# A squared-ReLU MLP on one core: other load order, transposes and transfer sizes at the start

## The chip, the cores and the metric

The kernel runs on one core of one Trainium2 chip. The metric is the device time of one launch in microseconds. The times before are eight runs with a median of 291.09 us (290.92 to 291.54).

## What is computed

```python
B, S, D, F = 1, 2048, 576, 4608      # all inputs bf16
h = jnp.einsum("bsd,df->bsf", x, w1) + b1
r = jnp.where(h > 0, h, 0)
h = r * r
out = jnp.einsum("bsf,fd->bsd", h, w2) + b2
```

So each of 2048 rows of x (576 columns) goes through w1 (576 x 4608), a bias, ReLU, a square, w2 (4608 x 576) and a second bias.

## The kernel before

The 2048 rows are worked in four blocks `sb` of 512 rows. TensorE contracts over partitions, so x is wanted transposed: `xT_blk[sb]` holds nine windows of 128 partitions x 512 rows. Windows O to O+3 hold the four full slices of 128 columns, E3 the last 128 columns (448 to 575). `dup_windows` (L117 to L120) copies them with partitions 0 to 63 and 64 to 127 exchanged, so that every slice of 64 columns is found in both halves of the partitions; VectorE does it in two copies.

The hidden columns (36 tiles of 128) are split. The first four tiles (G = 4) are done by `a_full`, with w1 held as `w1n` (four chunks k of 128 rows x 512 columns) and `w1n8` (the last 64 rows of w1). The other 32 are done by `a_rows` in 16 steps j; each step runs two matmuls of 64 rows side by side, nine times (L188, L190), from `w1_h`, which holds two column halves h = 0 and 1 in partitions 0 to 63 and 64 to 127. After a PSUM bank is full, `evac_h` takes it: ScalarE adds b1 (`b1T`) and applies ReLU (L176), VectorE squares (L177). When two blocks are done, `phase_t` computes the last 128 output columns transposed (L270), and `phase_b` the first 448 (L289), both from `w2_sb`.

Only block 0 makes its own transposes, on TensorE, since it must start at once. Blocks 1 to 3 are transposed by DMA (`load_xT`).

The start, in the order of the code: seven warm matmuls on constants (L63, 3200 columns in all); x row tiles and w1n chunks are loaded, x tiles 1 and 2 from ScalarE's queue, the rest from SyncE's (L71 to L92); POOL makes `ident`, clears `b1_rows` and loads b1 and the end of b2 with its own DMAs (L95 to L102); ScalarE loads its activation table at L104. Then `a_full(0, "k_outer")` works in halves of 256 rows: `x_transpose(j, k)` (L145 to L149) puts a slice of x tile j into a PSUM bank, `x_copies(h)` (L151 to L159) brings one half's five slices to SBUF (three copies on VectorE, two on ScalarE), and `part(h, k)` (L224 to L229) multiplies one slice of one half with four column tiles of w1n. The order of these calls (L231 to L250) is TensorE's order. `make_b1T` (L164 to L167) transposes b1 in between, and `pair` (L202 to L206) adds the last 64 rows of w1. Then `a_rows(0, 12, 1)` begins; at its step 12 the windows of block 1 are copied.

SyncE's queue runs in the order of the code as well: the w1 columns in pairs h = 0, 1 for the steps j in (0,1), (1,2), (2,4), ... (10,12), with w1n8 after the first pair; the transposed x of block 1; columns (12,14), (14,16); b2 spread to all partitions; w2 in six transfers of six row tiles; x of blocks 2 and 3. `keep` holds the written order on each engine. In the build, the DMAs from SyncE and ScalarE take eight semaphores in turn, so that each one from the ninth on is issued only when the eighth before it has landed.

PSUM has eight banks: four in the pool `ps_h` and four in `ps_o`. Before, the transposes of block 0 use six of them, two banks of which are used for both halves.

Of the kernel before, what the change touches and what calls it, by code (L numbers as in the profile page):

```python
# [11 lines left out]
BF16 = mybir.dt.bfloat16  # L12
FP32 = mybir.dt.float32
# [4 lines left out]
def kernel(  # L18
# [9 lines left out]
    nc = tc.nc  # L28
    keep = tc.keep_in_program_order
    P = 128  # L30
    H = 64
    x2 = x.flatten_outer_dims()
    out2 = out.flatten_outer_dims()
    S, D = x2.shape
    F = w1.shape[1]
    NFT = F // P
    NC = D // H
    NK = NC // 2
    G = 4
    GW = G * P  # L40
# [6 lines left out]
    DM = D - DT  # L47

    const = ctx.enter_context(tc.tile_pool(name="const", bufs=1))
    wpool = ctx.enter_context(tc.tile_pool(name="wpool", bufs=1))  # L50
# [5 lines left out]
    ps_h = ctx.enter_context(tc.tile_pool(name="ps_h", bufs=4, space=PSUM))  # L56
    ps_o = ctx.enter_context(tc.tile_pool(name="ps_o", bufs=4, space=PSUM))

    wps = ps_o.tile([P, 512], FP32, name="wps", tag="po")
    ones = nc.const_aps.tensor(1.0, [P, 512], BF16)  # L60
    WARM = [512] * 6 + [128]
    for i, n in enumerate(WARM):
        keep(nc.tensor.matmul(wps[:, 0:n], lhsT=ones[:, 0:P], rhs=ones[:, 0:n], start=True, stop=True))  # L63

    xs = const.tile([P, RT, D], BF16, name="x_sb")
    w1n = wpool.tile([P, NK, GW], BF16, name="w1n")
    w1n8 = wpool.tile([P, G // 2, P], BF16, name="w1n8")
    w1_h = wpool.tile([P, NC, FH], BF16, name="w1_h")
    w1_v = w1.rearrange("(c p) f -> p c f", p=H)

    def load_x(eng, rt):  # L71
        keep(eng.dma_start(out=xs[:, rt, :], in_=x2[rt * P:(rt + 1) * P, :]))

    def load_w1n(eng, k):
        keep(eng.dma_start(out=w1n[:, k, :], in_=w1[k * P:(k + 1) * P, 0:GW]))

    def load_w1n8(eng, h):
        src = w1[NK * P:D, 0:GW].rearrange("p (i h f) -> p i h f", h=2, f=P)
        keep(eng.dma_start(out=w1n8[h * H:(h + 1) * H, :, :], in_=src[:, :, h, :]))

    def load_w1(eng, h, j0, j1):
        keep(eng.dma_start(out=w1_h[h * H:(h + 1) * H, :, j0 * P:j1 * P],
                      in_=w1_v[:, :, GW + h * FH + j0 * P:GW + h * FH + j1 * P]))

    load_x(nc.sync, 0)
    load_x(nc.scalar, 1)
    load_w1n(nc.sync, 0)
    load_x(nc.scalar, 2)
    load_w1n(nc.sync, 1)
    load_x(nc.sync, 3)  # L90
    for k in range(2, NK):
        load_w1n(nc.sync, k)  # L92

    ident = const.tile([P, P], BF16, name="ident")
    make_identity(nc, ident[:])  # L95
    b1_rows = const.tile([P, P], BF16, name="b1_rows")
    nc.gpsimd.memset(b1_rows[:], 0.0)
    nc.gpsimd.dma_start(out=b1_rows[0:NFT, :], in_=b1.rearrange("(ft p) -> ft p", p=P))
    b2_col = const.tile([P, 1], BF16, name="b2_col")
    nc.gpsimd.dma_start(out=b2_col[:], in_=b2[DM:D].rearrange("(d o) -> d o", o=1))  # L100
    b2T = const.tile([P, 1], FP32, name="b2T")
    nc.gpsimd.tensor_copy(out=b2T[:], in_=b2_col[:])  # L102
    warm = const.tile([P, 1], FP32, name="warm")
    keep(nc.scalar.activation(out=warm[:], in_=nc.const_aps.tensor(0.0, [P, 1], FP32), func=ACT.Relu))  # L104

    E3, O, SPC, E = 0, 1, 5, 6
    LO_W = [O, O + 1, O + 2, O + 3, E, E + 1, E + 2, E3, SPC]
# [20 lines left out]

    w2_sb = wpool.tile([P, NFT, D], BF16, name="w2_sb")
    w2_view = w2.rearrange("(ft p) d -> p ft d", p=P)  # L130
    W2CH = 6

    def load_w2(c):
        keep(nc.sync.dma_start(out=w2_sb[:, c * W2CH:(c + 1) * W2CH, :], in_=w2_view[:, c * W2CH:(c + 1) * W2CH, :]))
# [3 lines left out]
    alloc_xT(0)  # L138
    xT0 = xT_blk[0]
    HS = SB // 2  # L140
    tb_po = [ps_o.tile([P, 2, HS], BF16, name="tb", tag="po") for _ in range(2)]
    tb_ph = [ps_h.tile([P, 2, HS], BF16, name="tb", tag="ph") for _ in range(4)]
    half_banks = [tb_ph, None]

    def x_transpose(j, k):  # L145
        h, q = divmod(j, 2)
        qc = slice(q * P, (q + 1) * P)
        bank, slot, c0 = (half_banks[h][k], 0, k * P) if k < NK else (half_banks[h][2], 1, D - P)
        keep(nc.tensor.transpose(bank[:, slot, qc], xs[:, j, c0:c0 + P], ident[:]))  # L149

    def x_copies(h):  # L151
        hc = slice(h * HS, (h + 1) * HS)
        for k in range(NK):
            src = half_banks[h][k][:, 0, :]
            if k % 2 == 0:
                keep(nc.vector.tensor_copy(out=xT0[:, O + k, hc], in_=src))  # L156
            else:
                keep(nc.scalar.copy(out=xT0[:, O + k, hc], in_=src))
        keep(nc.vector.tensor_copy(out=xT0[:, E3, hc], in_=half_banks[h][2][:, 1, :]))  # L159


    b1T = const.tile([P, NFT], FP32, name="b1T")

    def make_b1T():  # L164
        b1T_ps = ps_o.tile([P, P], BF16, name="b1T_ps", tag="po")
        keep(nc.tensor.transpose(b1T_ps[:], b1_rows[:], ident[:]))  # L166
        keep(nc.vector.tensor_copy(out=b1T[:], in_=b1T_ps[:, 0:NFT]))  # L167

# [26 lines left out]
    def a_full(sb, order):  # L195
        xT = xT_blk[sb]
        banks = []
        for g in range(G):
            pool, tag = (ps_o, "po") if g < 2 else (ps_h, "ph")
            banks.append(pool.tile([P, SB], FP32, name="pn", tag=tag))  # L200

        def pair(i, start, stop):  # L202
            keep(nc.tensor.matmul(banks[2 * i][:], lhsT=w1n8[0:H, i, :], rhs=xT[0:H, SPC, :],  # L203
                             start=start, stop=stop, skip_group_check=order == "k_outer"))
            keep(nc.tensor.matmul(banks[2 * i + 1][:], lhsT=w1n8[H:P, i, :], rhs=xT[H:P, E3, :],  # L205
                             start=start, stop=stop, skip_group_check=order == "k_outer"))  # L206

        def full(g, k, start, stop):
            keep(nc.tensor.matmul(banks[g][:], lhsT=w1n[:, k, g * P:(g + 1) * P], rhs=xT[:, O + k, :],  # L209
                             start=start, stop=stop))  # L210

        if order == "rows_first":
            for i in (1, 0):
                pair(i, True, False)
            for g in (2, 3, 0, 1):
                for k in range(NK):
                    full(g, k, False, k == NK - 1)
                evac_h(sb, banks[g], g)
        else:
            if order == "k_outer":  # L220
                tb_new = [ps_h.tile([P, 2, HS], BF16, name="tb", tag="ph") for _ in range(2)]
                half_banks[1] = tb_new + tb_po

                def part(h, k):  # L224
                    hc = slice(h * HS, (h + 1) * HS)
                    for g in range(G):
                        keep(nc.tensor.matmul(banks[g][:, hc], lhsT=w1n[:, k, g * P:(g + 1) * P],  # L227
                                              rhs=xT[:, O + k, hc], start=(h == 0 and k == 0), stop=False,
                                              skip_group_check=True))  # L229

                for j in range(2):  # L231
                    for k in range(NK):
                        x_transpose(j, k)
                for j in range(2):
                    x_transpose(j, NK)
                x_copies(0)
                part(0, 0)
                for k in range(NK + 1):
                    x_transpose(2, k)
                part(0, 1)  # L240
                part(0, 2)
                for k in range(NK + 1):
                    x_transpose(3, k)
                x_copies(1)
                dup_windows(0)
                part(0, 3)
                part(1, 0)
                make_b1T()
                for k in range(1, NK):
                    part(1, k)  # L250
            else:
                for g in (2, 3, 0, 1):
                    for k in range(NK):
                        full(g, k, k == 0, False)
            for i in (1, 0):
                pair(i, False, True)
                evac_h(sb, banks[2 * i], 2 * i)
                evac_h(sb, banks[2 * i + 1], 2 * i + 1)
# [35 lines left out]
    for (j0, j1) in [(0, 1), (1, 2), (2, 4), (4, 6), (6, 8), (8, 10), (10, 12)]:  # L294
        load_w1(nc.sync, 0, j0, j1)
        load_w1(nc.sync, 1, j0, j1)
        if j0 == 0:
            load_w1n8(nc.sync, 0)
            load_w1n8(nc.sync, 1)
    load_xT(1)  # L300
    for (j0, j1) in [(12, 14), (14, 16)]:
        load_w1(nc.sync, 0, j0, j1)
        load_w1(nc.sync, 1, j0, j1)
    keep(nc.sync.dma_start(out=b2_bc[:], in_=b2.partition_broadcast(P)))
    for c in (0, 3, 1, 4, 2, 5):
        load_w2(c)
    load_xT(2)

    alloc_hT(0)
    a_full(0, "k_outer")  # L310
    a_rows(0, 12, 1)
    alloc_hT(1)
# [47 lines left out]
```

## Time and profile before

| what | value |
|---|---|
| median of eight runs | 291.09 us |
| profiled execution, own time | 291.17 us |
| its span in the profile | 289.4 us (1.77 us of the time lie outside) |
| DMA, whole span | 16.52 MB, mean 57 GB/s |
| DMA share from 0 to 3.8 us, and to 4.9 | 0.55, then 0.93 |
| first row matmul (L188) | at 9.79 us |
| TensorE from 10 to 20 us | busy 10.00 us |
| w1 columns, 288 KB each | 14 issues, median 6.1 us to landing |
| w2, 864 KB each | 6 issues, median 9.9 us to landing |

The times inside the profile count from the start of its span. PE is TensorE, PEld its weight loads, DVE VectorE, ACT ScalarE, SP SyncE; an engine's name with a q is its sequencer, which issues DMAs. A line of the timeline has the start, the length, the engine, the line of the kernel, the operation, what it writes and reads, the number of instructions, and in brackets the idle time before them with what ended it. Matmul ends are modelled; the distance between two starts tells the rate.

### The profile page before, as it was taken

The page shows a single profiled execution, that of the slowest core. Times are in us where ns is not written, and L with a number is a line of the kernel's source. Part 1 is how long each engine was busy: PE and PEld are TensorE (multiplying, and loading weights), DVE is VectorE, ACT ScalarE, POOL GpSimd, SP SyncE. Part 2 cuts the span into 40 slices and gives each one's busy share as a digit, 9 for nine tenths or more (in the row PEclk, how much of TensorE's full clock was granted, in tenths as well). Part 3 has the DMA queues.
Part 4 walks back from the last instruction along what each step waited for, and adds up shares of the span by engine and source line. Part 5 has one row for each costly group of instructions (what it writes and reads, how often), then busy time and mean ns, then how long its engine had stood idle before and what let it go on. Part 6 is the DMA issues. An engine that isn't in the chain of part 4 may idle for free.

```text
span 289.4 us, 4699 instructions
## 1 busy us (share of the span) xinstructions
PE 285.3 (99%) x2032; PEld 139.4 (48%) x2032; DVE 78.6 (27%) x176; ACT 96.7 (33%) x154; POOL 2.3 (1%) x10
## 2 busy tenths in 40 slices
PE   8999999999999999999999999999999999999995
PEld 5544444444444555555544444444444455555554
DVE  1644544444500200000025444444440001100001
ACT  3666666766500000000027666666770000000000
POOL 3000000000000000000000000000000000000000
DMA  7999999200001100000000000000000110000000
GB/s 195 223 250 197 321 386 222 61 0 2 0 18 33 39 16 18 16 16 18 16 16 2 1 2 0 2 0 2 0 2 0 36 39 16 16 17 32 19 16 18
DMA packets 31638, 16.52 MB, mean 57 GB/s; under 512 B 15733, under 2 KB 31617, under 8 KB 31617
## 3 DMA queue, kind: packets, MB, share of 16 engines
q1 hardware_dynamic: 31264, 15.91, 21.6%
q10 hardware_dynamic: 288, 0.30, 0.4%
q8 instruction: 16, 0.26, 0.4%
q14 instruction: 6, 0.04, 0.0%
q0 software_dynamic: 64, 0.01, 0.0%
HBM read 11.36 MB, written 2.36 MB: 47 GB/s over the span
## 4 chain that ended last, share of the span: by engine, by line
PE 98%; DMA 1%; DVE 0%; issue 0%
PE ph L188 42%; PE po L289 38%; PE pt L270 11%; PE pn L209 4%; PE pn L227 1%; DMA x_sb<-in_x_dram 1%; PE tb L149 1%; PE ph L190 1%; PE pn L203 1%; DVE o_sb L291 0%; PE b1T_ps L166 0%; PE pn L205 0%
## 5 line engine op out<-in xcount | busy, mean ns | idle before, releaser
L188 PE MATMUL ph<-xTw,w_h 64*128 64x512 bf16 x576 | 124.6, 376 | 0.0
L190 PE MATMUL ph<-xTw,w_h 64*128 64x512 bf16 x576 | 124.6, 376 | 0.0
L289 PE MATMUL po<-w_sb,hT 128*128 128x448 bf16 (+2 forms) x612 | 109.4, 341 | 0.0
L176 ACT ACTIVATE r<-ph,b1T 128x512 bf16<-128x512 f32 x128 | 81.1, 685 | 41.6 <-PE ph L190 41.6
L188 PEld LDWEIGHTS <-w_h 64*128 64x128 bf16 x576 | 54.1, 94 | 68.1
L289 PEld LDWEIGHTS <-hT 128*128 128x128 bf16 x612 | 58.5, 98 | 51.0
L177 DVE TENSOR_TENSOR hT<-r 128x512 bf16<-128x512 bf16 x144 | 61.2, 426 | 75.8 <-ACT r L176 75.2
L190 PEld LDWEIGHTS <-w_h 64*128 64x128 bf16 x576 | 54.1, 94 | 0.0
L291 DVE TENSOR_TENSOR o_sb<-po,b_bc 128x448 bf16<-128x448 f32 (+2 forms) x17 | 10.2, 597 | 125.8 <-PE po L289 125.8
L270 PE MATMUL pt<-hT,w_sb 128*128 128x512 bf16 x144 | 31.4, 379 | 0.0
L176 ACT ACTIVATE r<-pn,b1T 128x512 bf16<-128x512 f32 x16 | 10.3, 688 | 61.0 <-PE pn L205 59.6
L270 PEld LDWEIGHTS <-w_sb 128*128 128x128 bf16 x144 | 14.1, 98 | 17.0
L273 ACT ACTIVATE oT<-pt,b2T 128x512 bf16<-128x512 f32 x4 | 2.8, 688 | 28.3 <-PE pt L270 28.3
L209 PE MATMUL pn<-xTw,w1n 128*128 128x512 bf16 x48 | 10.9, 379 | 0.0
L209 PEld LDWEIGHTS <-w1n 128*128 128x128 bf16 x48 | 4.5, 98 | 6.0 <-issue 0.8
L227 PE MATMUL pn<-xTw,w1n 128*128 128x256 bf16 x32 | 4.0, 272 | 0.0
L63 PE MATMUL wps<-const-bfloat16-1.0 128*128 128x512 bf16 (+1 forms) x7 | 2.8, 578 | 0.8 <-PEq L344 0.8
L227 PEld LDWEIGHTS <-w1n 128*128 128x128 bf16 x32 | 3.0, 99 | 0.3
L119 DVE COPY xTw<-xTw 64x2048 bf16<-64x2048 bf16 x4 | 2.8, 690 | 0.2
L156 DVE COPY xTw<-tb 128x256 bf16<-128x256 bf16 x4 | 1.1, 292 | 6.2 <-PE tb L149 6.2
L120 DVE COPY xTw<-xTw 64x2048 bf16<-64x2048 bf16 x4 | 2.8, 688 | 0.1
L149 PE MATMUL tb<-ident,x_sb 128*128 128x128 bf16 x20 | 2.3, 263 | 0.3 <-DMA x_sb<-in_x_dram 0.2
(23 smaller groups left out, 14.9 us busy)
## 6 DMA issues: line engine op xcount, KB each, us to landing
w_sb<-in_w_dram SPq DMA_DIRECT2D x6, 864.0 KB, 9.9
w_h<-in_w_dram SPq DMA_DIRECT2D x14, 288.0 KB, 6.1
out_dram<-o_sb SPq DMA_DIRECT2D x15, 112.0 KB, 1.7
w_h<-in_w_dram SPq DMA_DIRECT2D x4, 144.0 KB, 3.4
w1n<-in_w_dram SPq DMA_DIRECT2D x4, 128.0 KB, 3.3
out_dram<-ot SPq DMA_DIRECT2D x4, 128.0 KB, 2.0
x_sb<-in_x_dram ACTq DMA_DIRECT2D x2, 144.0 KB, 2.9
x_sb<-in_x_dram SPq DMA_DIRECT2D x2, 144.0 KB, 3.3
```

What stands on the lines that cost most here:

```text
L63: keep(nc.tensor.matmul(wps[:, 0:n], lhsT=ones[:, 0:P], rhs=ones[:, 0:n], start=True, stop=True))
L149: keep(nc.tensor.transpose(bank[:, slot, qc], xs[:, j, c0:c0 + P], ident[:]))
L176: keep(nc.scalar.activation(out=r[:], in_=bank[:], func=ACT.Relu, bias=b1T[:, ft:ft + 1], scale=1.0))
L177: keep(nc.vector.tensor_tensor(out=hTs[sb][:, ft, :], in0=r[:], in1=r[:], op=ALU.mult))
L188: keep(nc.tensor.matmul(bx[:], lhsT=w1_h[0:H, LO_C[i], jc], rhs=xT[0:H, LO_W[i], :], start=(i == 0), stop=(i == NC - 1)))
L190: keep(nc.tensor.matmul(by[:], lhsT=w1_h[H:P, UP_C[i], jc], rhs=xT[H:P, UP_W[i], :], start=(i == 0), stop=(i == NC - 1)))
L203: keep(nc.tensor.matmul(banks[2 * i][:], lhsT=w1n8[0:H, i, :], rhs=xT[0:H, SPC, :], start=start, stop=stop, skip_group_check=order == "k_o ...
L209: keep(nc.tensor.matmul(banks[g][:], lhsT=w1n[:, k, g * P:(g + 1) * P], rhs=xT[:, O + k, :], start=start, stop=stop))
L227: keep(nc.tensor.matmul(banks[g][:, hc], lhsT=w1n[:, k, g * P:(g + 1) * P], rhs=xT[:, O + k, hc], start=(h == 0 and k == 0), stop=False, s ...
L270: keep(nc.tensor.matmul(pt[:], lhsT=w2_sb[:, ft, DM:D], rhs=hT[:, ft, :], start=(i == 0), stop=(i == NFT - 1)))
L289: keep(nc.tensor.matmul(po[:, 0:d1 - d0], lhsT=hT[:, ft, jj * P:(jj + 1) * P], rhs=w2_sb[:, ft, d0:d1], start=(i == 0), stop=(i == NFT - 1)))
L291: keep(nc.vector.tensor_tensor(out=o_sb[:, d0:d1], in0=po[:, 0:d1 - d0], in1=b2_bc[:, d0:d1], op=ALU.add))
```

## The change

The x row tiles 0 and 1 are loaded in two column pieces each (0 to 255, and 256 to 575), on SyncE and ScalarE. Then w1n chunks go on SyncE and x tiles 2 and 3 on ScalarE in turn; chunk 3 goes on ScalarE. b1 is loaded from ScalarE's queue after its activation table; `b1_rows` is cleared by VectorE; the end of b2 is loaded from SyncE's queue after the w1 columns. Both halves of w1n8 now hold all 512 columns and are loaded before the first w1 columns. The transposes have four banks of their own, all in `ps_h`, and each slice is copied out as soon as its second row tile is transposed; two of the ten copies are on ScalarE. Block 0's four accumulators all lie in `ps_o`. The order on TensorE becomes: slices 0 and 1 of x tiles 0 and 1, then their other three slices, one `part`, x tile 2, one `part`, x tile 3, and the rest. The w1 columns (12,14) and (14,16) become one pair (12,16), and w2 comes in two transfers of 18 row tiles in place of six of six. There are six warm matmuls with 2816 columns in all.

```diff
-    wps = ps_o.tile([P, 512], FP32, name="wps", tag="po")
+    wps = ps_h.tile([P, 512], FP32, name="wps", tag="ph")
-    WARM = [512] * 6 + [128]
+    WARM = [512] * 5 + [256]
...
-    w1n8 = wpool.tile([P, G // 2, P], BF16, name="w1n8")
+    w1n8 = wpool.tile([P, GW], BF16, name="w1n8")
...
+    def load_x(eng, rt, c0=0, c1=D):
+        keep(eng.dma_start(out=xs[:, rt, c0:c1], in_=x2[rt * P:(rt + 1) * P, c0:c1]))
...
     def load_w1n8(eng, h):
-        src = w1[NK * P:D, 0:GW].rearrange("p (i h f) -> p i h f", h=2, f=P)
-        keep(eng.dma_start(out=w1n8[h * H:(h + 1) * H, :, :], in_=src[:, :, h, :]))
+        keep(eng.dma_start(out=w1n8[h * H:(h + 1) * H, :], in_=w1[NK * P:D, 0:GW]))
...
-    load_x(nc.sync, 0)
-    load_x(nc.scalar, 1)
-    load_w1n(nc.sync, 0)
-    load_x(nc.scalar, 2)
-    load_w1n(nc.sync, 1)
-    load_x(nc.sync, 3)
-    for k in range(2, NK):
-        load_w1n(nc.sync, k)
+    b1_rows = const.tile([P, P], BF16, name="b1_rows")
+    nc.vector.memset(b1_rows[:], 0.0)
+    for c0, c1 in [(0, 2 * P), (2 * P, D)]:
+        load_x(nc.sync, 0, c0, c1)
+        load_x(nc.scalar, 1, c0, c1)
+    for k in range(2):
+        load_w1n(nc.sync, k, k + 1)
+        load_x(nc.scalar, 2 + k)
+    load_w1n(nc.sync, 2, 3)
+    load_w1n(nc.scalar, 3, 4)
...
-    b1_rows = const.tile([P, P], BF16, name="b1_rows")
-    nc.gpsimd.memset(b1_rows[:], 0.0)
-    nc.gpsimd.dma_start(out=b1_rows[0:NFT, :], in_=b1.rearrange("(ft p) -> ft p", p=P))
-    b2_col = const.tile([P, 1], BF16, name="b2_col")
-    nc.gpsimd.dma_start(out=b2_col[:], in_=b2[DM:D].rearrange("(d o) -> d o", o=1))
-    b2T = const.tile([P, 1], FP32, name="b2T")
-    nc.gpsimd.tensor_copy(out=b2T[:], in_=b2_col[:])
     warm = const.tile([P, 1], FP32, name="warm")
     keep(nc.scalar.activation(out=warm[:], ...))
+    keep(nc.scalar.dma_start(out=b1_rows[0:NFT, :], in_=b1.rearrange("(ft p) -> ft p", p=P)))
+    for h in range(2):
+        load_w1n8(nc.sync, h)
...
-    W2CH = 6
+    W2CH = 18
...
-    tb_po = [ps_o.tile([P, 2, HS], BF16, name="tb", tag="po") for _ in range(2)]
-    tb_ph = [ps_h.tile([P, 2, HS], BF16, name="tb", tag="ph") for _ in range(4)]
+    tb = [[ps_h.tile([P, 4, HS], BF16, name="tb", tag="ph") for _ in range(2)] for _ in range(2)]
+    PLACE = [(0, 0), (0, 1), (1, 0), (1, 1), (0, 2)]
+    T_ORDER = [0, 1, 2, 3, NK]
+
+    def x_transpose(j, ks=T_ORDER):
+        h, q = divmod(j, 2)
+        hc = slice(h * HS, (h + 1) * HS)
+        for k in ks:
+            bank, slot = PLACE[k]
+            c0 = k * P if k < NK else D - P
+            keep(nc.tensor.transpose(tb[h][bank][:, slot, q * P:(q + 1) * P], xs[:, j, c0:c0 + P], ident[:]))
+            if q == 1:
+                w = O + k if k < NK else E3
+                if h == 1 and bank == 1:
+                    keep(nc.scalar.copy(out=xT0[:, w, hc], in_=tb[h][bank][:, slot, :]))
+                else:
+                    keep(nc.vector.tensor_copy(out=xT0[:, w, hc], in_=tb[h][bank][:, slot, :]))
...
-        b1T_ps = ps_o.tile([P, P], BF16, name="b1T_ps", tag="po")
+        b1T_ps = ps_h.tile([P, P], BF16, name="b1T_ps", tag="ph")
...
-            pool, tag = (ps_o, "po") if g < 2 else (ps_h, "ph")
+            pool, tag = (ps_o, "po") if g < 2 or order == "k_outer" else (ps_h, "ph")
...
-                for j in range(2):
-                    for k in range(NK):
-                        x_transpose(j, k)
-                for j in range(2):
-                    x_transpose(j, NK)
-                x_copies(0)
-                part(0, 0)
-                for k in range(NK + 1):
-                    x_transpose(2, k)
-                part(0, 1)
-                part(0, 2)
-                for k in range(NK + 1):
-                    x_transpose(3, k)
-                x_copies(1)
+                for ks in (T_ORDER[:2], T_ORDER[2:]):
+                    for j in range(2):
+                        x_transpose(j, ks)
+                for k in range(2):
+                    part(0, k)
+                    x_transpose(2 + k)
                 dup_windows(0)
-                part(0, 3)
+                for k in range(2, NK):
+                    part(0, k)
                 part(1, 0)
                 make_b1T()
...
     for (j0, j1) in [(0, 1), (1, 2), (2, 4), (4, 6), (6, 8), (8, 10), (10, 12)]:
         load_w1(nc.sync, 0, j0, j1)
         load_w1(nc.sync, 1, j0, j1)
-        if j0 == 0:
-            load_w1n8(nc.sync, 0)
-            load_w1n8(nc.sync, 1)
     load_xT(1)
-    for (j0, j1) in [(12, 14), (14, 16)]:
+    for (j0, j1) in [(12, 16)]:
         load_w1(nc.sync, 0, j0, j1)
         load_w1(nc.sync, 1, j0, j1)
+    b2_col = const.tile([P, 1], BF16, name="b2_col")
+    keep(nc.sync.dma_start(out=b2_col[:], in_=b2[DM:D].rearrange("(d o) -> d o", o=1)))
+    b2T = const.tile([P, 1], FP32, name="b2T")
+    nc.gpsimd.tensor_copy(out=b2T[:], in_=b2_col[:])
     keep(nc.sync.dma_start(out=b2_bc[:], in_=b2.partition_broadcast(P)))
-    for c in (0, 3, 1, 4, 2, 5):
+    for c in range(2):
         load_w2(c)
     load_xT(2)
```

More of the change, by code (lines that the diff above doesn't have):

```diff
@@ L66, with load_w1n @@
     w1n = wpool.tile([P, NK, GW], BF16, name="w1n")
-    w1n8 = wpool.tile([P, G // 2, P], BF16, name="w1n8")
+    w1n8 = wpool.tile([P, GW], BF16, name="w1n8")
     w1_h = wpool.tile([P, NC, FH], BF16, name="w1_h")
     w1_v = w1.rearrange("(c p) f -> p c f", p=H)
[L71 to L75, printed above, removed]
+    def load_x(eng, rt, c0=0, c1=D):
+        keep(eng.dma_start(out=xs[:, rt, c0:c1], in_=x2[rt * P:(rt + 1) * P, c0:c1]))
+    def load_w1n(eng, k0, k1):
+        src = w1[k0 * P:k1 * P, 0:GW].rearrange("(k p) f -> p k f", p=P)
+        keep(eng.dma_start(out=w1n[:, k0:k1, :], in_=src))
     def load_w1n8(eng, h):
-        src = w1[NK * P:D, 0:GW].rearrange("p (i h f) -> p i h f", h=2, f=P)
-        keep(eng.dma_start(out=w1n8[h * H:(h + 1) * H, :, :], in_=src[:, :, h, :]))
+        keep(eng.dma_start(out=w1n8[h * H:(h + 1) * H, :], in_=w1[NK * P:D, 0:GW]))
     def load_w1(eng, h, j0, j1):
@@ L140 @@
     HS = SB // 2
-    tb_po = [ps_o.tile([P, 2, HS], BF16, name="tb", tag="po") for _ in range(2)]
-    tb_ph = [ps_h.tile([P, 2, HS], BF16, name="tb", tag="ph") for _ in range(4)]
-    half_banks = [tb_ph, None]
-    def x_transpose(j, k):
+    tb = [[ps_h.tile([P, 4, HS], BF16, name="tb", tag="ph") for _ in range(2)] for _ in range(2)]
+    PLACE = [(0, 0), (0, 1), (1, 0), (1, 1), (0, 2)]
+    T_ORDER = [0, 1, 2, 3, NK]
+    def x_transpose(j, ks=T_ORDER):
         h, q = divmod(j, 2)
[L147 to L151, printed above, removed]
         hc = slice(h * HS, (h + 1) * HS)
-        for k in range(NK):
[L154 to L159, printed above, removed]
+        for k in ks:
[8 more added lines that the diff above has]
+                    keep(nc.vector.tensor_copy(out=xT0[:, w, hc], in_=tb[h][bank][:, slot, :]))
     b1T = const.tile([P, NFT], FP32, name="b1T")
     def make_b1T():
-        b1T_ps = ps_o.tile([P, P], BF16, name="b1T_ps", tag="po")
+        b1T_ps = ps_h.tile([P, P], BF16, name="b1T_ps", tag="ph")
         keep(nc.tensor.transpose(b1T_ps[:], b1_rows[:], ident[:]))
@@ L198, in a_full @@
         for g in range(G):
-            pool, tag = (ps_o, "po") if g < 2 else (ps_h, "ph")
+            pool, tag = (ps_o, "po") if g < 2 or order == "k_outer" else (ps_h, "ph")
             banks.append(pool.tile([P, SB], FP32, name="pn", tag=tag))
         def pair(i, start, stop):
-            keep(nc.tensor.matmul(banks[2 * i][:], lhsT=w1n8[0:H, i, :], rhs=xT[0:H, SPC, :],
+            keep(nc.tensor.matmul(banks[2 * i][:], lhsT=w1n8[0:H, 2 * i * P:(2 * i + 1) * P], rhs=xT[0:H, SPC, :],
                              start=start, stop=stop, skip_group_check=order == "k_outer"))
-            keep(nc.tensor.matmul(banks[2 * i + 1][:], lhsT=w1n8[H:P, i, :], rhs=xT[H:P, E3, :],
+            keep(nc.tensor.matmul(banks[2 * i + 1][:], lhsT=w1n8[H:P, (2 * i + 1) * P:(2 * i + 2) * P], rhs=xT[H:P, E3, :],
                              start=start, stop=stop, skip_group_check=order == "k_outer"))
@@ L220, in a_full @@
             if order == "k_outer":
-                tb_new = [ps_h.tile([P, 2, HS], BF16, name="tb", tag="ph") for _ in range(2)]
-                half_banks[1] = tb_new + tb_po
                 def part(h, k):
@@ L229, in part @@
                                               skip_group_check=True))
-                for j in range(2):
-                    for k in range(NK):
-                        x_transpose(j, k)
-                for j in range(2):
-                    x_transpose(j, NK)
-                x_copies(0)
-                part(0, 0)
-                for k in range(NK + 1):
-                    x_transpose(2, k)
-                part(0, 1)
-                part(0, 2)
-                for k in range(NK + 1):
-                    x_transpose(3, k)
-                x_copies(1)
+                for ks in (T_ORDER[:2], T_ORDER[2:]):
[4 more added lines that the diff above has]
+                    x_transpose(2 + k)
                 dup_windows(0)
-                part(0, 3)
+                for k in range(2, NK):
+                    part(0, k)
                 part(1, 0)
```

## The prediction

> **What bounds the kernel now.** I read the page first. TensorE is busy almost throughout, while the DMA queues and ScalarE have room:
>
> ```profile
> PE 285.3 (99%) x2032; PEld 139.4 (48%) x2032; DVE 78.6 (27%) x176; ACT 96.7 (33%) x154; POOL 2.3 (1%) x10
> ...
> PE 98%; DMA 1%; DVE 0%; issue 0%
> ```
>
> The change takes no row matmul, no L289 and no L270 away. What it can move is the head, before the w1 rows (L188) begin, or a load that the rows come to wait for. The chain of waits shows the head in order of time (start, length, what):
>
> ```profile
> 0.73 3.04 DMA x_sb<-in_x_dram
> 3.83 1.22 PE tb L149 x10
> 5.04 0.48 PE pn L227 x4
> 5.62 0.40 PE tb L149 x4
> 6.02 0.87 PE pn L227 x8
> 6.90 0.28 PE tb L149 x5
> 7.17 0.87 PE pn L227 x8
> ```
>
> TensorE waits for x to 3.83. The first ten transposes take 0.107 us each, the later five of L149 (6.90 to 7.17) only 0.056: the first ten run at half rate. From 4.92 the 128x256 matmuls start 0.109 us apart. The timeline gives the rest: TensorE idles from 5.38+ to 5.62 for a free bank, and again before 9.35, because VectorE's window copies (L119, L120) end at 9.22.
>
> ```profile
> 5.62 0.23 PEld L149 LDWEIGHTS <-x_sb 128*128 128x128 bf16 x4 [0.28 <-DVE xTw L159]
> ...
> 8.53 0.69 DVE L120 COPY xTw<-xTw 64x2048 bf16<-64x2048 bf16 x1
> ...
> 9.34 0.09 PEld L203 LDWEIGHTS <-w1n 64*128 64x128 bf16 x1 [0.21 <-issue]
> ```
>
> The last view is the timeline of SyncE beside the rows. Rows start at 9.79; each j takes 9 x 0.216 = 1.94 us, so j=2 starts at 13.68. It needs the w1 columns (2,4), which SP issues at 7.72 (h=0, partitions 0 to 63) and 8.40 (h=1, the other 64):
>
> ```profile
> 7.72 0.64 SPq L82 DMA_DIRECT2D w_h<-in_w_dram  x1
> 8.40 0.64 SPq L82 DMA_DIRECT2D w_h<-in_w_dram  x1
> ...
> 13.46 0.38 PE L190 MATMUL ph<-xTw,w_h 64*128 64x512 bf16 x1
> 13.58 0.09 PEld L190 LDWEIGHTS <-w_h 64*128 64x128 bf16 x1
> ```
>
> The DMA view of short windows gives 4.7 and 5.1 us to landing for those two, so 12.4 and 13.5. The weight load at 13.58 lies 0.12 behind its usual place: the chunk comes a tenth of a microsecond ahead of need. So the head has two bounds close together: TensorE's own work, and the supply of w1 columns (2,4). The next pair (issued 9.09 and 9.77) lands by about 15.7 and is needed at 17.56.
>
> **What the skill says.** "TensorE: Matmul & The Clock Gate", part on the HAM clock gate: the array starts at half clock, 107 against 56 ns for 128 columns, and turns to full after some 4 us of activity. The trace agrees: 0.107, then 0.056, and the turn lies at about 4.9, 4.1 us after the first warm matmul at 0.78. The page adds that the window runs freely, so the turn can shift. "DMA: Bandwidth & Descriptors", section on issuing engines: transfers from SP and ACT run on the same 16 DMA engines, so a second queue saves only issue time. The trace agrees in size: 0.40 to 0.47 us per issue. "ScalarE: Activation LUTs", on what a table load costs: 1283 ns, from a backing slot filled earlier. The trace has 1.28, so I take it as unaffected by DMA traffic.
>
> **The change, part by part.**
>
> *First x pieces.* Before, x tiles 0 and 1 (2 x 144 KB) are issued at 0.73 and landed by 3.77; packets flow from 1.76 and 0.27 MB are through by 3.0. Columns 0 to 255 of both are 131 KB, through by about 2.6 to 2.7 in the same traffic; with the 0.65 us from last packet to landing (3.77 less 3.1) that is 3.3. The warm matmuls shrink from 3200 to 2816 columns at 0.83 ns, ending the issue at about 3.2, so they don't stand in the way. Four transposes from 3.3 take 0.43. The other pieces (295 KB in all, plus 256 more packets than before) land at about 3.9, and six transposes end at 4.55. That is 0.35 earlier, all at half rate, so worth 0.18; the four following matmuls get another 0.3 us of half-rate time, worth 0.15.
>
> *Bank and window stalls.* Four own PSUM banks for the transposes remove the 0.24 at 5.38. The second transposes (j=3) come one group of four matmuls earlier, so L119/L120 end 0.6 before the pair needs them, where they were 0.13 late. VectorE now has eight copies at 0.29 and ScalarE two at 0.376; five copies of half 0 are hidden under the first two matmul groups. Sum of the head if nothing else comes late: 0.18 + 0.15 + 0.24 + 0.13 = 0.70, less about 0.2 of small gaps between pieces and waits for w1n = 0.5. Rows would start at 9.29.
>
> *Issue order and waits.* In both builds hardware DMAs take eight semaphores in turn, so each issue from the ninth on waits until the eighth before it has landed. Before, SP's own 0.4 to 0.7 us per issue was slower than that. Now the split makes two more transfers early, so w1n chunk 2 (SP) waits for x piece 0 (3.3, where it was issued at 2.65), chunk 3 (ACT) for x piece 1 (3.3, was 3.13). Queued behind chunk 2 are both w1n8 and all w1 columns; behind chunk 3 are the table load and b1.
> - Chunks 2 and 3: issued 3.3, landing 2.6 (nearest, less the cold start of the first x) to 3.4 us later (chunk 2 before), 5.9 to 6.7; needed at 6.17 and 6.6. I take 6.1; cost 0, at most 0.45.
> - w1n8 (64x512 twice, 131 KB instead of 64 KB): issued 3.9 and 4.35 after x's second pieces; each about 0.4. Landing 2.5 to 3.1 later, needed at 8.85: hidden.
> - w1 columns: j=0 h=0 at 4.8, h=1 waits for x tile 3 (ACT issue 2.1, plus 3.5, so 5.5). Then 0.68 per issue: j=1 at 6.2 and 6.85, columns (2,4) at 7.55 and 8.2. j=0 h=1 lands 3.6 later at 9.1, just in time. (2,4) h=1 lands 5.1 later at 13.3, while rows from 9.29 would need it at 13.17. So j=2 starts at about 13.45 instead of 13.68, and all later rows shift by that: a gain of 0.23, not 0.5.
> - b1: ACT issues chunk 3 to 3.7, table load to 5.0, warm activation 0.2, b1 at 5.25. A small load took 2.5 to 3.1 on SP in traffic; with an almost empty ACT ring I allow 1.9 to 3.3: 7.15 to 8.55. TensorE's in-order transpose (L166) needs it at 7.5, and twelve matmuls, the pairs and all rows are queued behind it. I take 7.5: no cost; the top costs 1.05 at that place. b2_col moves to the SP queue behind the last w1; it is used after 91 us.
>
> *Later loads.* Columns (12,16) come as one pair of 576 KB: issued at about 23.5, 1.18 MB at 250 to 390 GB/s (rates at 14-18 and 38-42) from 25.7, landing by 29.5 to 31.4; needed at j=12, 32.7. Hidden by 1.3 at the least. w2 in two transfers of 18 row tiles (the code has 18) moves the same bytes; before, SP was through issuing them at 38.4 and loads ended by 54, first use 75.9. Hidden by 20 us; b2_bc and the x transposes behind it are as far from use. POOL loses two DMAs of which none waits. Cost nothing, bounds plus or minus 0.05.
>
> Sum: the gain of 0.23 is seen at j=2. Against the profiled execution's own 291.17 (span 289.4 and 1.77 around it) that is 290.94. Its time lies 0.08 over the median 291.09, so I say 290.9. A measurement can tell about 0.2%, 0.58 us, from no change.
>
> **Rivals.**
> *Full gain.* Columns (2,4) land by 13.1 because the DMA engines start fuller; then 0.5 (up to 0.7) stays: 290.5. For it: DMA share was only 0.71 to 0.86 from 5.8 to 9.4. Against: the issue time of h=1 hardly moves (8.40 to 8.2). 0.25.
> *b1 comes late, slower.* The wait on x piece 1 holds ACT, then 1.28 and 0.2 stand ahead of b1's issue. It decides from a landing of about 7.95 on: then the rows start later than 9.79. At 8.55 rows start at 10.35, 0.55 later: 291.65. The same sign comes if x tile 3 lands at 6.0, since h=1 of column 0 waits for it. For it: w1n8's second half took 2.5 us and column 0 took 3.6 in that traffic. Against: ACT's ring holds nothing else by then. 0.22.
> *The change doesn't do what it says:* the x pieces land no earlier since packets, not bytes, set the start (256 packets either way). Then only the stalls vanish, and (2,4) sets the end anyway: 291.0, within the forecast's own range.
>
> **Numbers.** Forecast, 290.5 to 291.3 around 290.9: 0.53. Full gain 0.25, slower case 0.22. Below -0.58 lies about half of the full gain's case, 0.13; above +0.58 some four fifths of the slower case, 0.18, since a late b1 also pushes chunks; the rest, 0.69, is no measurable change. Range 290.4 to 291.6, which cuts the ends of both rivals.
>
> **What would show it.** First transpose at 3.2 to 3.4; no wait of L149 on VectorE; chunk 2's issue at about 3.3; b1's landing against its transpose; a gap on TensorE ahead of row j=2 ended by w_h; first row at 9.2 to 9.5. The forecast is wrong if a gap ahead of b1's transpose exceeds 0.4, if w1 columns after (2,4) or (12,16) end a gap, or if the clock turns far from 4.9.

## The result and the profile after

| | before | after |
|---|---|---|
| median | 291.23 us (290.87 to 291.75, 32 runs) | 293.19 us (292.23 to 295.48, 12 runs) |
| ratio to before | | 1.0066, 95% interval 1.0053 to 1.008 |
| profiled execution, own time | 291.17 us | 293.55 us |
| span | 289.4 us | 291.8 us |
| first transpose | 3.83 | 3.07 |
| first row matmul | 9.79 | 12.54 |

The kernel became slower by 1.9 us, against a forecast of 0.2 us less (290.9 against 291.09). The runs after lie in groups (292.2 to 292.8, 293.6, and one of 295.5), which those of before don't. The profiled execution, on which the lines below rest, is one of the middle group.

The first part of the page after, and its chain of waits up to the rows (start, length, what):

```profile
PE 286.6 (98%) x2031; PEld 140.1 (48%) x2031; DVE 79.5 (27%) x179; ACT 96.2 (33%) x152; POOL 0.9 (0%) x7
```

```profile
3.28 0.33 PE tb L149 x3
3.64 0.30 DVE xTw L155
4.29 0.30 DVE xTw L155
4.63 0.39 PE tb L149 x2
5.04 0.30 DVE xTw L155
5.38 0.37 PE tb L149 x2
5.75 0.85 PE pn L219 x4
6.61 0.53 PE tb L149 x5
7.14 0.85 PE pn L219 x4
8.14 0.30 DVE xTw L155
8.48 0.29 PE tb L149 x2
8.79 0.38 ACT xTw L153
9.49 1.31 PE pn L219 x12
```

Two things are new. Copies out of PSUM (L155 on VectorE, L153 on ScalarE) now stand in the chain between transposes; before, none did. And groups of four 128x256 matmuls take 0.85 us (0.213 each) at 5.75 and at 7.14, where they took 0.48 at 5.04 and 0.87 for eight at 6.02 before: the half rate lasts beyond 8 us instead of to 4.9. The timeline names the waits:

```profile
3.98 0.48 PE L149 MATMUL tb<-ident,x_sb 128*128 128x128 bf16 x3 [0.38 <-DVE xTw L155]
...
4.63 0.37 PE L149 MATMUL tb<-ident,x_sb 128*128 128x128 bf16 x2 [0.17 <-DVE xTw L155]
...
5.38 0.37 PE L149 MATMUL tb<-ident,x_sb 128*128 128x128 bf16 x2 [0.38 <-DVE xTw L155]
...
8.48 0.27 PE L149 MATMUL tb<-ident,x_sb 128*128 128x128 bf16 x2 [0.38 <-DVE xTw L155]
...
9.21 0.27 PE L149 MATMUL tb<-ident,x_sb 128*128 128x128 bf16 x2 [0.46 <-ACT xTw L153]
...
12.54 0.38 PE L183 MATMUL ph<-xTw,w_h 64*128 64x512 bf16 x1
```

The bracket counts from the modelled end of the transpose before. By the distance of starts, the five waits (ahead of 3.98, 4.63, 5.38, 8.48 and 9.21) take 0.59, 0.37, 0.59, 0.59 and 0.62 us, 2.76 in all. A transpose is done, the copy waits for it some 0.35, copies for 0.29, and only then may TensorE write the next slice into the same bank. "PSUM — Partial Sum Buffer", section on bank collisions, says why the build puts a wait there at all: TensorE writing and another engine reading the same bank at once is an error that the hardware doesn't arbitrate. The waits agree with that; no run here tried it without.

The sum of the head, from the first transpose to the first row: 9.47 us after, 5.96 before. Both hold 5.1 us of work at full pace (20 x 0.056, 32 x 0.109, 0.056, two pairs at 0.216). Half rate adds 1.65 after (16 transposes x 0.051, eight matmuls x 0.104) and 0.51 before (ten transposes); the rest, 2.7 after and 0.35 before, is idle. So the rows begin later by 2.4 (idle) + 1.1 (half rate) - 0.76 (transposes begin earlier) = 2.75. The span grows by 2.4, since the stretch from the last add to its end is 0.35 shorter.

### The profile page after: what moved, and what is told of

It is laid out like the page before. It is cut to its first block, busy times and chain, and to the rows that moved or that the text cites. A ratio compares the mean times of both kernels' runs of the same rounds, so it can differ in the third digit from the quotient of the medians.

```text
span 291.8 us, 4694 instructions
## 1 busy us (share of the span) xinstructions
PE 286.6 (98%) x2031; PEld 140.1 (48%) x2031; DVE 79.5 (27%) x179; ACT 96.2 (33%) x152; POOL 0.9 (0%) x7
## 4 chain that ended last, share of the span: by engine, by line
PE 98%; DVE 1%; issue 0%; ACT 0%
PE ph L183 42%; PE po L274 37%; PE pt L255 11%; PE pn L204 4%; PE pn L219 1%; PE tb L149 1%; PE wps L63 1%; PE ph L185 1%; PE pn L198 1%; DVE xTw L155 0%; ACT xTw L153 0%; DVE o_sb L276 0%; PE b1T_ps L161 0%; PE pn L200 0%
## 5 line engine op out<-in xcount | busy, mean ns | idle before, releaser
L255 PE MATMUL pt<-hT,w_sb 128*128 128x512 bf16 x144 | 31.4, 379 | 0.0
L149 PE MATMUL tb<-ident,x_sb 128*128 128x128 bf16 x20 | 3.3, 286 | 1.8 <-DVE xTw L155 1.3
L219 PE MATMUL pn<-xTw,w1n 128*128 128x256 bf16 x32 | 5.0, 309 | 0.0
L155 DVE COPY xTw<-tb 128x256 bf16<-128x256 bf16 x8 | 2.2, 291 | 6.6 <-PE tb L149 6.6
L149 PEld LDWEIGHTS <-x_sb 128*128 128x128 bf16 x20 | 2.3, 133 | 3.2 <-issue 2.0
L117 DVE COPY xTw<-xTw 64x2048 bf16<-64x2048 bf16 x4 | 2.8, 690 | 0.2
(20 smaller groups left out, 13.4 us busy)
```

The source lines that it names most:

```text
L149: keep(nc.tensor.transpose(tb[h][bank][:, slot, q * P:(q + 1) * P], xs[:, j, c0:c0 + P], ident[:]))
L255: keep(nc.tensor.matmul(pt[:], lhsT=w2_sb[:, ft, DM:D], rhs=hT[:, ft, :], start=(i == 0), stop=(i == NFT - 1)))
```

## The experiments

**Copies behind the transposes, and each side of the change alone.** Four kernels with one set of questions: is it the banks (theory A) or the loads (theory B), and does the clock follow from the gaps? The first expectation states both theories. Ratios are to the kernel before throughout, with a 95% interval behind them; first rows and turns of the clock are those of one profiled execution.

*e1_copies_after*, the kernel after with copies behind all transposes of a half:

```diff
-            if q == 1:
-                w = O + k if k < NK else E3
-                ...
+    def x_copies(h, ks=T_ORDER):
+        ...
                 for ks in (T_ORDER[:2], T_ORDER[2:]):
                     for j in range(2):
                         x_transpose(j, ks)
+                x_copies(0)
                 for k in range(2):
                     part(0, k)
                     x_transpose(2 + k)
+                x_copies(1)
```

> The kernel after, with one thing changed: the copies of a half are issued behind all ten transposes of that half, so that no transpose writes a PSUM bank that a copy still has to read. Loads, banks and the order of transposes and matmuls stay. Theory A (transposes wait for copies of the same bank, five times in the head, and the idle time also delays the turn of TensorE's clock): the waits are gone, the clock turns at about 5 us, the first row starts at 9.5 to 9.9 instead of 12.54, time 290.9 to 291.4. Theory B (the loads: the DMA issues that wait for a landing, and b1 behind the table load): nothing of that is changed, so the time stays within 292.2 to 293.7.

Measured: 292.78 (six runs, 291.82 to 293.35), ratio 1.0051 (1.0036 to 1.0067). The five waits are gone and the first row starts at 10.08, near what theory A said. Half rate ends early, between 3.4 and 3.6 by the pace of the transposes, but then TensorE waits for w1n chunk 0, which the x pieces ahead of it put from an issue at 1.20 to one at 1.65:

```profile
5.43 0.61 PE L222 MATMUL pn<-xTw,w1n 128*128 128x256 bf16 x4 [1.33 <-DMA w1n<-in_w_dram]
```

The time is not what theory A said; it lies in the range of theory B. A new wait stands in the rows. The waits in the window from 9 to 40 us, and the weight loads around step j=12:

```profile
PE ph L188 <- DMA w_h<-in_w_dram: 1.4, 1, 1.4
```

```profile
33.18 0.09 PEld L186 LDWEIGHTS <-w_h 64*128 64x128 bf16 x1
35.17 0.09 PEld L188 LDWEIGHTS <-w_h 64*128 64x128 bf16 x1 [1.90 <-DMA w_h<-in_w_dram]
```

That is the second half of columns (12,16). The weights come 1.78 late (35.17 against 33.39), and from row start to the last add this execution is 1.8 longer than before's. So theory A held for the bank waits of the head, and a second loss lay behind it.

*e2_loads_only*: the loads after, everything on TensorE and PSUM as before.

```diff
-    tb = [[ps_h.tile([P, 4, HS], ...) for _ in range(2)] for _ in range(2)]
+    tb_po = [ps_o.tile([P, 2, HS], BF16, name="tb", tag="po") for _ in range(2)]
+    tb_ph = [ps_h.tile([P, 2, HS], BF16, name="tb", tag="ph") for _ in range(4)]
...
+    x_transpose, x_copies and the order of a_full as before
```

> The loads and their order as after, shorter warm-up as after, but transposes, copies, PSUM banks and TensorE's order as before. Theory A: no wait on a shared bank, first row at 9.4 to 9.8, time 290.7 to 291.3. Theory B: as slow as after, 292.2 to 293.7.

Measured: 293.49 (291.87 to 293.68), ratio 1.0064 (1.0045 to 1.0083), first row at 12.35. Theory A wanted this kernel fast, as it has no bank waits; it is as slow as theory B said, so the loads have a loss of their own. Its timeline shows ScalarE's copies behind b1's issue:

```profile
5.12 0.74 ACTq L100 DMA_DIRECT2D b_rows<-in_b_dram  x1
...
5.90 0.65 ACT L156 COPY xTw<-tb 128x256 bf16<-128x256 bf16 x2 [0.98 <-DVE xTw L157]
```

*e3_transposes_only*: the loads before, transposes, banks and order after.

```diff
-    tb_po = [ps_o.tile([P, 2, HS], ...) for _ in range(2)]
-    tb_ph = [ps_h.tile([P, 2, HS], ...) for _ in range(4)]
+    tb, PLACE, T_ORDER, x_transpose and the order of a_full as after
```

> The loads as before, but transposes, copies, PSUM banks and TensorE's order as after. Theory A: the waits are all there and begin later, since x lands at 3.77 whole: first row at 12 to 13, time 292.5 to 294. Theory B: as before, 290.9 to 291.5.

Measured: 293.2 (292.94 to 294.64), ratio 1.0079 (1.006 to 1.0099), first row at 13.27 (its profiled execution is the slowest of its six, 294.64). As theory A said: the transposes alone cost as much, with the loads of before, and the five waits are all there.

*e4_fill*: the kernel after with transposes of the identity in the gaps.

```diff
     T_ORDER = [0, 1, 2, 3, NK]
+    FILL = {(1, 1): 5, (0, NK): 4, (1, 3): 5}
...
+            for _ in range(FILL.get((j, k), 0)):
+                keep(nc.tensor.transpose(tb[1][1][:, 3, 0:P], ident[:], ident[:]))
```

> The kernel after, with 14 transposes of the identity (into an unused part of a bank) put into the three gaps of the first half, 5, 4 and 5 of them; the waits on the copies stay. It tells the two parts of theory A apart. If the idle gaps delay the clock's turn: the turn comes at about 5 instead of 8 us, the matmuls after it take 0.109 instead of 0.213 us, the first row comes about 1.1 us earlier (11.3 to 11.6), time 292.0 to 292.5 with a small spread. If only the waits count and the clock's turn does not depend on the gaps: 293.2 and up, spread as after. Theory B: no change but for some 0.2 us.

Measured: 292.71 (292.21 to 292.87), ratio 1.0045 (1.0032 to 1.0057), first row at 11.69. The chain shows full pace from 6.1 on:

```profile
5.85 0.63 PE pn L222 x4
...
6.76 0.44 PE pn L222 x4
```

The time lies between the two expectations, and the interval still overlaps that of after (1.0053 to 1.008). What sets them apart are the slow runs: with *e15_fill_pairs* below, which has the same head, all eleven runs with fillers took at most 292.89, while six of the twelve of after took 293.6 or more. In the profiled executions the first row comes 0.85 us earlier, though TensorE does more work. So the gaps do delay the clock's turn. What is left, 1.9 us at the first row against before, is not the waits alone: the fillers last a little longer than the gaps (the first matmul starts at 5.64 instead of 5.55), and the turn at 6.13 is still later than that of before.

**The late transfers by themselves.**

```diff
-    for (j0, j1) in [(12, 14), (14, 16)]:
+    for (j0, j1) in [(12, 16)]:          # e5_pair, on the kernel before
...
-    W2CH = 6
+    W2CH = 18                            # e5_w2, on the kernel before
```

> The kernel before with one edit: the w1 columns (12,14) and (14,16) as one pair (12,16). Theory C (the pair lands after step j=12 of the rows starts, and the kernel after only hides it because its rows start 2.75 us later): a wait on w_h ahead of j=12 at about 33.1 us, 0.3 to 1.8 us long, time 291.6 to 293. Rival, as predicted: the pair lands by 31.4, no wait, 291.0 to 291.4.

> The kernel before with one edit: w2 in two transfers of 18 row tiles. It is first used at 76 us. All theories: no wait on it, 291.0 to 291.4. A slower time would mean that the large transfers hold up something else.

*e5_pair*: 291.25 (13 runs), ratio 1.0003 (0.9994 to 1.0011). The profiled execution has the wait that theory C names, the weight load being 0.72 late (33.47 against 32.75):

```profile
32.54 0.09 PEld L188 LDWEIGHTS <-w_h 64*128 64x128 bf16 x1
33.47 0.09 PEld L190 LDWEIGHTS <-w_h 64*128 64x128 bf16 x1 [0.83 <-DMA w_h<-in_w_dram]
```

In that execution the rows had begun at 9.45, 0.34 earlier than in the one of before, which hides part of it; in the median the pair costs nothing that can be told. So it is at its limit there: theory C's place is right, its price on the kernel before was not. *e5_w2*: 291.0 (14 runs), ratio 0.9992 (0.9983 to 1.0): nothing lost, as all theories said.

*e6_copies_pairs*: e1 with the late columns in two pairs.

```diff
-    for (j0, j1) in [(12, 16)]:
+    for (j0, j1) in [(12, 14), (14, 16)]:     # on e1_copies_after
```

> The kernel of e1_copies_after with the w1 columns (12,14) and (14,16) in pairs of their own again. Theory C: the wait of 1.4 us at 33 us goes, what is left is the first row at 10.08 against 9.79, so 291.3 to 291.7. If instead the supply of w1 as a whole is late in these loads: the wait stays in part, 292 to 292.8.

Measured: 291.31 (14 runs, 290.73 to 293.35), ratio 1.0019 (1.0001 to 1.0036), no wait on w_h. So the pair cost e1 about 0.9 us by the ratios, whose intervals just touch. Four of the 14 runs took 292.9 to 293.4, though.

**Is it the clock? Gaps made and filled.** *e10_loads_b1_pool* takes b1 off ScalarE in e2, and splits the late pair.

```diff
-    keep(nc.scalar.dma_start(out=b1_rows[0:NFT, :], ...))
+    keep(nc.gpsimd.dma_start(out=b1_rows[0:NFT, :], ...))
```

> The kernel of e2_loads_only with b1 loaded from POOL as before, and with the w1 columns (12,14), (14,16) in pairs of their own. Theory D (in e2 the two copies on ScalarE stand behind b1's DMA issue, which waits for w1n chunk 0; that idles TensorE at 5.9 and delays its clock): ScalarE copies at about 4.8, the clock turns at about 5, first row at 9.5 to 10.0, time 290.8 to 291.5. If ScalarE's queue is not the cause: first row at 12 and more, 292.5 to 293.7.

Measured: 293.14 (292.92 to 293.23), ratio 1.0065 (1.0053 to 1.0077), first row at 11.88. ScalarE copied at 4.65, as theory D wanted, and the time hardly moved: theory D fell. What is left is this, in the timeline and the chain:

```profile
4.00 1.03 PE L147 MATMUL tb<-ident,x_sb 128*128 128x128 bf16 x8 [0.51 <-DMA x_sb<-in_x_dram]
```

```profile
6.19 0.53 PE tb L147 x5
6.73 1.71 PE pn L225 x8
8.43 0.53 PE tb L147 x5
```

TensorE waits for the second x pieces (third transpose in the order of before). After it comes one shorter wait, for w1n chunk 0 (to 5.16), and the later work runs at half rate to beyond 9 us.

So I formed theory E, from the traces and "TensorE: Matmul & The Clock Gate", part on the HAM clock gate, which says that the monitor looks at free-running windows of 3413 ns. The traces agree with the length: in eleven of them the granted full clock is on record, and it lasts 279.893, 283.306 or 286.720 us, which is 82, 83 or 84 times 3.413. Theory E says that the turn comes at the end of the first window in which TensorE was busy enough. The table gives the busy share (columns of the matmuls times their pace, 0.833 ns a column at half rate) of the window that ends with the turn, and of those before it, the nearest first. The trace of before has no clock on record; its turn is read from the pace of the matmuls:

| kernel, profiled execution | turn at | busy in the window it ends | busy in the windows before it |
|---|---|---|---|
| before | 4.93 | 0.86 | 0.22 |
| after | 8.12 | 0.76 | 0.72 |
| e2_loads_only | 9.82 | 0.98 | 0.53, 0.65 |
| e3_transposes_only | 8.69 | 0.78 | 0.62 |
| e4_fill | 6.13 | 0.97 | 0.57 |
| e5_w2 | 3.63 | 0.79 | |
| e6_copies_pairs | 6.19 | 0.81 | 0.58 |
| e10_loads_b1_pool | 9.45 | 1.0 | 0.69, 0.54 |

Every window of 0.76 or more ends in the turn, none of 0.72 or less does. In the kernel after, the window from 1.29 to 4.71 holds two of the waits (0.59 and 0.37) and falls short by little; that costs a whole window more at half rate. Where the windows lie differs from execution to execution (before, modulo 3.413, 1.52; e5_w2, 0.22), which would explain that one kernel has several times; the clock is on record for the profiled executions alone.

*e11_fill_x_gap* and *e12_short_warm* test it from both sides:

```diff
+                        if j == 0 and k == 2:                  # e11, on e10
+                            for _ in range(7):
+                                keep(nc.tensor.transpose(half_banks[0][3][:, 1, 0:P], ident[:], ident[:]))
...
-    WARM = [512] * 6 + [128]                                   # e12, on the kernel before
+    WARM = [512] * 3
```

> The kernel of e10_loads_b1_pool with seven transposes of the identity in the 0.8 us in which TensorE waits for the second x pieces. Theory E (the clock turns at the end of a free-running stretch of 3.4 us if TensorE was busy in more than about three quarters of it; in e10 the wait for the pieces makes one stretch fall short, and the turn comes 3.4 us later): the turn comes by 6.9 at the latest, first row at 9.7 to 10.9, median 291.2 to 292. If the idle time has no say in the turn: as e10, 293.1.

> The kernel before with three warm matmuls of 512 columns instead of seven, so that TensorE idles from about 2.1 to 3.8 us. All loads and all work stay as they are. Theory E: stretches that hold this idle time fall short, so the turn comes between 7 and 9 us, the head's matmuls run at half rate until then, first row at 11 to 12.5, time 292.3 to 293.7, with no new wait anywhere. If the turn only depends on where the first matmul lies: as before, 291.0 to 291.5.

*e11*: 291.55 (21 runs), ratio 1.0013 (1.0003 to 1.0023); turn at 5.94, first row at 10.37. Seven useless transposes take 1.5 us off e10 by the ratios. *e12*: 292.51 (291.64 to 292.83), ratio 1.0039 (1.0027 to 1.0051); turn at 8.63, the window before it busy to 0.46, first row at 11.33, and the chain has no new wait, only half pace:

```profile
3.72 1.25 PE tb L149 x10
4.97 0.95 PE pn L227 x4
5.91 0.53 PE tb L149 x5
6.45 1.71 PE pn L227 x8
```

Theory E held in both. Where the windows lie does not explain it, as each kernel has them nearly where its partner has (modulo 3.413: e10 2.62, e11 2.52; before 1.52, e12 1.80). What differs is how busy they are: the window of 0.69 in e10 has 0.86 in e11, that of 0.86 in before has 0.46 in e12.

**Does the late pair cost anything in the kernel after?** *e14_after_pairs* is the kernel after with the late columns split, *e15_fill_pairs* is e4_fill with them split (the same edit as in e6).

> The kernel after, with the w1 columns (12,14) and (14,16) in pairs of their own again. Theory C (the late pair is hidden as long as the rows start 2.75 us later): as after, 292.2 to 293.7, median 292.8 to 293.3. If the pair costs by itself: 0.5 to 1.5 us faster than after.

Measured: 295.62 (293.9 to 295.88), ratio 1.0133 (1.011 to 1.0156). Neither expectation. The head is that of after to 8.5 us, but in this execution the windows end at 6.57, 9.98 and 13.40, the first two are busy to 0.55 and 0.63, and the turn comes only with the third, so that twelve matmuls more, and about half of the next twelve, run at half rate:

```profile
9.68 2.56 PE pn L219 x12
```

It says nothing on the pair; it shows how far the clock can push this head (first row at 14.60). Why none of its six runs was as fast as the median of after, with the same head, stays open: for the other five the clock is not on record.

> The kernel of e4_fill (the waits on shared banks stay, the gaps of the first half are filled, so that the clock's turn scatters less) with the w1 columns (12,14) and (14,16) in pairs of their own. Theory C (the late pair is hidden while the rows start 1.9 us late): as e4, 292.2 to 292.9. If the late pair cost something in the kernel after: 0.4 us or more below e4. If the split pairs themselves made e14 slow: above 293.5.

Measured: 292.54 (292.37 to 292.89), ratio 1.0042 (1.0027 to 1.0056), as e4's 1.0045: with rows that begin at 11.7, the late pair costs nothing. Theory C's hiding holds.

**All three mended, and a better version.** *e17_mended_fill* is e6 with seven transposes of the identity ahead of the first matmul group.

```diff
                 x_copies(0)
+                for _ in range(7):
+                    keep(nc.tensor.transpose(tb[1][1][:, 3, 0:P], ident[:], ident[:]))
```

> The kernel of e6_copies_pairs (copies behind all transposes, late columns in two pairs) with seven transposes of the identity in the gap in which TensorE waits for the first copy and w1n chunk 0. If shared banks, the clock's turn and the late pair are the whole loss of the kernel after: the runs of 293.2 that e6 has in 4 of 14 vanish, median 290.9 to 291.4, ratio 0.998 to 1.001. If something else is lost in these loads: ratio over 1.002.

Measured: 291.55 (22 runs, 290.92 to 292.88), ratio 1.0011 (1.0001 to 1.002), first row at 9.92. Its profiled execution is a fast one (291.1). Median and ratio both lie just above what I expected, and the ratio below the 1.002 of the other case; two of the 22 runs still took over 292.6. Against e6 (1.0019) the gain of the fillers is not clear of noise. With the three mended together, all but 0.0011 of the loss of 0.0066 is gone. What is left may be in part the wait for w1n chunk 0: e11 waits for it to 5.36, and here that group starts at 5.27, where before started it at 4.92. No run isolates this.

*e9_best* is the kernel before with other places for the slices of the second half, x tile 3 transposed earlier and w1n8 loaded from POOL (the last slice of the second half also shares another bank than before; that line is not shown):

```diff
-                half_banks[1] = tb_new + tb_po
+                half_banks[1] = tb_po + tb_new
...
-                for k in range(NK + 1):
+                for k in (0, 1, NK, 3, 2):
                     x_transpose(2, k)
                 part(0, 1)
-                part(0, 2)
...
                 dup_windows(0)
+                part(0, 2)
                 part(0, 3)
...
-            load_w1n8(nc.sync, 0)
-            load_w1n8(nc.sync, 1)
+    load_w1n8(nc.gpsimd, 0)
+    load_w1n8(nc.gpsimd, 1)
```

> A version meant to beat both: the kernel before, with x tile 2's slices placed so that TensorE does not wait for a bank at 5.4 us, x tile 3 transposed one group of matmuls earlier so that the window copies end in time, and w1n8 loaded from POOL, which brings w1 columns (2,4) forward on SP by 1.3 us. If the two stalls of 0.24 and 0.13 us are all there is: first row at 9.4 to 9.5, 290.8 to 290.9, ratio about 0.999. If the turn of the clock dominates, its scatter of about 0.5 us hides that.

Measured: 290.96 (22 runs, 290.52 to 291.58), ratio 0.9987 (0.998 to 0.9993), first row at 9.53. It is faster than before by 0.13%, and so than after by 0.8%. The transposes of x tile 2 follow the first group at once (before: 5.38 to 5.63 idle):

```profile
4.75 0.45 PE pn L229 x4
5.20 0.36 PE tb L151 x5
5.56 0.44 PE pn L229 x4
```

What the 0.13% come from is not shown, though. Those of x tile 3 now wait 0.19 for their landing (to 6.03), and from the first transpose (3.51) to the first row this execution takes 6.02 us, before took 5.96. Rows also began at 9.45 in e5_pair and at 9.61 in e5_w2, with the head of before unchanged.

## Why the prediction was wrong

*Bank and window stalls.* This step failed. It said that four banks of their own remove the stall of 0.24 and that the copies are hidden. It counted banks, not who shares one: slices 0, 1 and the last lie in one bank, 2 and 3 in the other, and each slice is copied out while the next is still to be written. The runs showed five waits of 2.76 us in place of the 0.24 (gone in e1, all there in e3). The prediction had named "no wait of L149 on VectorE" as a sign that it was right; four of the five are on VectorE, the last is on ScalarE.

*First x pieces.* The landing was better than I said: issued at 0.73, landed 2.1 us later, first transpose at 3.07 against 3.3. The 0.33 us from half-rate time were booked with the turn of the clock at 4.9. That was the second failure: the step took the turn as fixed, and named a turn far from 4.9 only among what would make it wrong. The waits put TensorE's idle time into the window that must be busy, and the turn came at 8.12 (that such gaps move it, e4, e11 and e12 show). In the profiled execution half rate cost 1.1 more instead of 0.33 less. A smaller miss: waits for w1n stood among "small gaps" of 0.2 in all, and where the bank waits are gone, chunk 0 alone stops TensorE for 1.33 (e1) and 0.44 (e6).

*Issue order and waits.* Chunk 2 is issued at 2.84, right when x piece 0 lands, chunk 3 at 3.02, and neither ends a gap. b1's transpose waits for nothing, being reached only at 10.6. But b1's issue held ScalarE's queue to 5.62 after and to 5.86 in e2, where two copies stood behind it; I had named what is queued behind chunk 3, not that b1 itself would wait for chunk 0's landing. The bound from columns (2,4), the core of the forecast, was never reached: with rows at 12.54 they were long there, and with rows at about 10 (e6, e17) no wait on them appears. Nor does one in e5_pair, which has the early loads of before and rows from 9.45, so that j=2 starts at 13.34. It was not shown to bind; in before, the weight load that came 0.12 late held up no matmul.

*Later loads.* w2 in two transfers costs nothing (e5_w2), as said. For columns (12,16) the landing was mis-sized: 31.4 at the latest, when e5_pair waited for it to 33.47 and e1 to 35.17. In the kernel after it costs nothing all the same, since the rows come 2.75 us later (e15).

*The rivals.* The slower one had the sign, for a reason that wasn't there: b1's transpose waited for nothing.

Left open: what the last 0.001 of e17 consists of, why e14 was slower than after, and whether the share at which the clock turns lies nearer 0.72 or 0.76.

## What to carry to other kernels

When tiles are packed into fewer PSUM banks, draw who writes and who reads each bank in order: a copy of one slice between the writes of two others turns a pipeline into a ping-pong of about 0.7 us a turn. At the start of a kernel, idle time on TensorE is not free even when other work hides it, as a window that falls short costs another 3.4 us at half rate, which is up to 1.7 us of work; fill it, or keep the warm-up dense up to the real work. And when a stall goes, ask which transfer was only hidden by it: mending the banks alone gave about two thirds of the gain back as a wait at 33 us (1.0051 in e1, 1.0019 in e6, from 1.0066).

## What the runs showed of the hardware

Useless work made kernels faster: seven transposes, 0.8 us of TensorE's time, took 1.5 us off (e11 against e10). The turn of the clock lay anywhere from 3.6 to 13.4 us in the traces that have it on record, and the busy share that decides it, as far as these show, between 0.72 and 0.76 of a 3.413 us window. A transfer of 128 x 512 B landed 2.1 to 2.3 us after its issue (after), one of 128 x 1152 B 2.9 to 3.0 (before), both at the head of an empty queue.
